# Attention into a routed mixture of experts: the hand-over between the two, and when the token lists of the experts are fetched

## The chip, the cores and the metric

One core of a Trainium2 chip runs the whole program. The metric is device time in microseconds; the times shown are three runs of the kernel before and one further execution under the profiler, from which all rows below are taken.

## The reference, cut to what matters

Attention with rotary positions over 8 batches, 8 heads, 576 tokens and 64 values per head gives 4608 rows of 512. Each row then goes to one of 8 experts, the one with the largest gate logit:

```python
q_rot, k_rot = rotate(q), rotate(k)
scores = matmul(q_rot, k_rot.T) / sqrt(64); attn = softmax(scores)
x = matmul(attn, v)                            # 4608 rows of 512
logits = x @ w_gate; e_idx = argmax(logits, 1) # 8 experts
gate_w = softmax(logits)[row, e_idx]
eom = sigmoid(x @ w_output_gate)
for e in range(8):
    mask = e_idx == e
    h = maximum(x[mask] @ w1[e], 0)            # 512 -> 1024
    out[mask] = gate_w[mask] * eom[mask, e] * (h @ w2[e])
```

## The kernel before, in words

**Attention.** The work goes over 32 pairs of heads (4 pairs in each of 8 batches). A pair has 9 steps g; each makes a block of scores (`scores`, L464 and L457, into the two buffers `sc`), its maximum (`peak`, L470 on VectorE), the exponential (`exp`, L479 on ScalarE) and a transpose (`turn`, L485 on VectorE). The product with v (`values`, L507 into `acc`), its copy (`evict`, L514 to L516), the turn back into rows together with the gate logits (`back`, L522) and the division (`divide`, L530 to L539, into `xb`) follow at fixed distances from the pair's first step, by the table EVENTS; there is one `acc` for all pairs. `att.at(g, k, f)` puts a function at step g, phase k, and `rest(cond)` runs what is left over after the last score step.

**Routing.** When a batch is finished, `place` finds each token's expert and its place in that expert's list: one-hot rows (`oh`, `ohb`), running sums over the token blocks (`ohs`, L620), a matrix product that counts (`s14`, L655), and two masks (`ro` on VectorE, `pl` on GpSimd, L685 and L687) whose product (`s20`, L695) adds token numbers into `lists` (`s21`, L698). The rows of x go to DRAM (`store`, L638 and L640, on the SP queue). For the last batch these functions come as a list of pieces.

**Experts.** The rows of the experts are worked in slots of 256 rows ("double") or 128 ("single"). Slots 0 to 4 are filled from the first six batches and can start before the last two are placed; list 0 gives their rows (`table0`), list 2 the next double slots and list 1 the single ones (`table1`). A list goes through the same function `slots`: it computes a row number, fetches the list by an indirect DMA from DRAM (L794, into `0tk`, `2tk`, `1tk`), waits some pieces, corrects it on VectorE (L801 to L804), turns it on TensorE (L808, `0tr`, `2tr`, `1tr`) and copies it to `idx` (L809). `gather` (L942, GpSimd queue) then fetches the rows of a slot into `xg`.

A slot has 8 steps j. In steps 0 to 3 TensorE multiplies the turned rows `xt` with a quarter of w1 (`products`, L1002, into `ph`, one of two buffers) and `first` takes the relu on ScalarE (L1019) and its low part on VectorE (L1020) into `ht`. In steps 4 to 7 it multiplies `ht` with a quarter of w2 (`second`, L1045, into `py`). Every weight block is split in two parts six steps ahead of its use (`split`: `wh` on ScalarE, L964, `wl` on VectorE or for some blocks GpSimd, L966), and loaded eight ahead (`load`, L955, SP queue). `turn` turns the rows of the next slot (L980 to L983) in steps 4 and 5; `store` scales and scatters the result (L1054 to L1057, GpSimd queue).

**Order.** Every engine runs its instructions in the order in which they are written. The left-over pieces of routing and of `table1` are put between the steps of the slots, two per step:

```python
left = att.last + pieces(moe.table1(), 60)
...
for _ in range(per):        # per = 2
    if left:
        left.pop(0)()
```

At the hand-over the kernel before turns the rows of slot 0 and makes its first two products once the `values` of the last pair (31) are written, then runs the rest of attention, then closes attention's pools and opens the experts' left pools. `ht` lies in the left pool, so `first` of steps 0 and 1 can only be written after that.

Of the kernel before, what the change touches and what calls it, by code (L numbers as in the profile page):

```python
# [117 lines left out]
def body(ctx, tc, nb, offs, qk, v, rope, cst, gates, w, out):  # L118
# [61 lines left out]
    if n0:  # L180
        g = att.done(nb - 3) + 1
        for k, f in enumerate(pieces(moe.table0(), 18)):
            att.at(g + k, 2, f)
        att.at(g + 18, 2, moe.fetch)
# [12 lines left out]
    if not n0:  # L197
        att.rest(lambda g: True)
        main.close()
        moe.open_right(pool(ctx, "mr", 1, side="right", reuse_waits="tile"))  # L200
        left = []
    else:

        att.rest(lambda g: g <= att.G + 1)
        for u in range(3):
            moe.split(u)
        att.rest(lambda g: g <= att.G + 8)
        for h in range(2):
            moe.turn(0, h)
        for j in range(2):  # L210
            moe.products(0, j)
        att.rest(lambda g: True)
        main.close()
    moe.open_left(pool(ctx, "ml", 1, side="left", reuse_waits="tile"),
                  pool(ctx, "ps_m", 1, space=PSUM, side="left", reuse_waits="tile"))
    if n0:
        left = att.last + pieces(moe.table1(), 60)
    else:
        for f in att.last + pieces(moe.table1(), 60):
            f()  # L220
        moe.fetch()
        moe.begin0()
        moe.begin1()
# [8 lines left out]
class Attention:  # L232
# [91 lines left out]
    def step(self, g):  # L324
        G, pairs = self.G, self.pairs
        part = lambda g: (pairs[g // 9], g % 9)
        if g < G:
            pr, i = part(g)
            if i == 0:
                pr.begin()  # L330
            pr.scores(i)
            pr.peak(i)
            pr.exp(i)
        self.now(g, 1)
        if 0 <= g - TURN < G:
            pr, i = part(g - TURN)
            pr.turn(i)
        self.now(g, 2)
        self.now(g, 3)
# [209 lines left out]
def place(tc, pools, pairs, b, NT, cc, trib, oneb, cnt, xbs, xd, row, lists):  # L549
# [155 lines left out]
    if last:  # L705
        return [s0, s1, s2, s3, s4, s5, s6, s7, lambda: (s8(), add0()), both(s9, 1), both(s10, 2), both(s11, 3), both(s12, 4),
                lambda: (s13(), stores(), base()), no, s14, no, s14b, s15, s16, s17, no] + [lambda c=c: ones(c) for c in range(NCH)] + [
                no, no, s20, no, s21, no]

# [15 lines left out]
class Moe:  # L725
# [3 lines left out]
    def __init__(self, tc, nb, pools, cc, ident, cnt, w, xd, lists, lst, out):  # L729
# [5 lines left out]
        self.idx, self.ei = {}, {}  # L735
        self.wr, self.wp, self.xt, self.ht, self.gss, self.pys, self.hrs, self.regs, self.phs = ({} for _ in range(9))

# [27 lines left out]

    def slots(self, n, m, ends, delta, first, step, wait):

# [36 lines left out]
        V.tensor_tensor(out=tk, in0=tk, in1=g, op=ALU.add)  # L804
        yield
        tr = self.small.tile(f"{n}tr2")
# [35 lines left out]
    def table0(self):  # L842
# [13 lines left out]
        yield  # L856
        yield from self.slots(0, 2 * self.n0, end, dl, None, 2, 5)

    def table1(self):
# [25 lines left out]
        if self.n2:  # L885
# [6 lines left out]
            d2 = self.starts("d2", g2, 0.0)  # L892
            yield from self.slots(2, 2 * self.n2, end, d2, g2[:, 0:1], 2, 5)
            yield
# [12 lines left out]
        d1 = self.starts("d1", g1, BIG)  # L907
        yield from self.slots(1, self.n1, e1, d1, g1[:, 0:1], 1, 5)
        self.used = t([1, 1], "used", I32)
# [47 lines left out]
    def split(self, u):  # L957
# [9 lines left out]
        self.wp[u] = (wh, wl)  # L967

    def turn(self, s, h):
        nc, V = self.nc, self.nc.vector  # L970
# [6 lines left out]
        xth, xtl = self.xt[s]  # L977
        tp = self.small.tile(f"mtp{s}_{h}{self.nm}")
        for dc in range(4):
            nc.tensor.transpose(out=tp[:, dc, :], in_=self.xgs[s % 2][:, h, dc * P:dc * P + P], identity=self.ident)  # L980
        hs = slice(h * P, h * P + P)
# [3 lines left out]
    def products(self, s, j):  # L985
        nc = self.nc
        xth, xtl = self.xt[s]
        wh, wl = (a.rearrange("p (d f) -> p d f", f=256) for a in self.wp.pop(8 * s + j))
        ph = self.phs[s, j] = self.ph.tile([P, 2, SLOT], F32, tag=f"ph{j % 2}", name=f"ph{s}_{j}{self.nm}")
        if self.todo[s][0] == 1:  # L990
            n = 0
            for dc in range(4):
                for st, mv in ((xth, wh), (xtl, wh), (xth, wl)):
                    nc.tensor.matmul(ph[:, 0, :], st[:, dc, 0:P], mv[:, dc, :], start=(n == 0), stop=(n == 11))  # L994
                    n += 1
            return
        for f in range(2):
            n = 0
            for dc in range(4):
                fs = slice(f * P, f * P + P)  # L1000
                for st, mv in ((wh, xth), (wh, xtl), (wl, xth)):
                    nc.tensor.matmul(ph[:, f, :], st[:, dc, fs], mv[:, dc, :], start=(n == 0), stop=(n == 11))  # L1002
                    n += 1

    def first(self, s, j):
        nc = self.nc
        fl = lambda a: a.rearrange("p a b -> p (a b)")
        if j == 0:
            self.ht[s] = [self.buf(f"ht{i}", 0, 1, 0, [P, 8, SLOT], F32R, f"ht{i}_{s}{self.nm}") for i in range(2)]
        hth, htl = self.ht[s]  # L1010
        js = slice(2 * j, 2 * j + 2)
        if (s, j) not in self.phs:
            self.products(s, j)
        ph = self.phs.pop((s, j))
        if self.todo[s][0] == 1:
# [68 lines left out]
    def slot(self, s, left, per=2):  # L1084
        for j in range(8):
            u = 8 * s + j
            single = self.todo[s][0] == 1
            if j < 4:
                self.first(s, j)
            else:  # L1090
                self.second(s, j - 4)
# [8 lines left out]
            if j == 6:  # L1100
                self.gather(s + 2)
            for _ in range(per):
                if left:
# [64 lines left out]
```

## Time and profile before

| | us |
|---|---|
| three runs | 1106.68, 1104.14, 1101.99 (median 1104.14) |
| the profiled execution | 1111.51 |
| its span, first to last instruction | 1109.7 |
| TensorE busy in the span | 1027.9 (93%) |
| VectorE busy | 827.9 (75%) |
| ScalarE busy | 644.7 (58%) |
| GpSimd busy | 604.1 (54%) |

Attention takes the first 575 us or so; the slots of the experts start at about 590. The share of busy time is an average over both; what counts in a stage is the wait that ends last there. The chain that ended last is 65% TensorE by its share of the span.

### The profile page before, as it was taken

The numbers are of one execution on the slowest core, as the hardware profiler recorded it, in microseconds if no ns is written. First come the engines' busy times: TensorE is split into PE (matmuls) and PEld (weight loads), VectorE is DVE, ScalarE is ACT, GpSimd is POOL, SyncE is SP. The second block draws the span as 40 slices with busy tenths as digits, with TensorE's granted clock in tenths as the row PEclk, the third lists the DMA queues.
The fourth block names the chain that finished last, engine by engine and source line by source line (L and its number), as shares of the span: only waits on it lengthen the run. The fifth ranks groups of instructions, "written<-read, shape, count | busy, mean of one in ns | idle before, by whom it ended". The sixth has DMA issues, their size and how long they took to land.

```text
span 1109.7 us, 34896 instructions
## 1 busy us (share of the span) xinstructions
PE 1027.9 (93%) x14465; PEld 890.5 (80%) x14465; DVE 827.9 (75%) x1357; ACT 644.7 (58%) x1345; POOL 604.1 (54%) x592
## 2 busy tenths in 40 slices
PE   3999999999999999999976998899999999999995
PEld 3788877877877787787766987798899889889885
DVE  6788888888888688788764775656767867876782
ACT  3466666666666465566453553455757756766772
POOL 4667887887978688688531051112532632632621
PEclk9999999999999899899888998999999999999998
DMA  5545555555746455545266585556887888888870
GB/s 184 162 129 164 167 165 145 152 166 159 199 126 174 114 167 173 130 145 159 51 184 210 199 302 184 190 171 193 301 291 252 286 286 292 265 305 304 256 274 27
DMA packets 58562, 216.48 MB, mean 195 GB/s; under 512 B 9405, under 2 KB 10012, under 8 KB 54304
## 3 DMA queue, kind: packets, MB, share of 16 engines
q1 hardware_dynamic: 50304, 194.03, 55.9%
q0 software_dynamic: 6496, 18.92, 4.8%
q8 instruction: 115, 1.88, 0.7%
q10 hardware_dynamic: 1600, 1.26, 0.4%
q14 instruction: 47, 0.39, 0.1%
HBM read 196.04 MB, written 20.24 MB: 195 GB/s over the span
## 4 chain that ended last, share of the span: by engine, by line
PE 65%; DVE 12%; issue 10%; DMA 6%; ACT 4%; POOL 2%; SPq 1%; POOLq 0%; ACTq 0%; DVEq 0%
PE py L1045 15%; PE sc L464 15%; PE acc L507 14%; PE ph L1002 11%; PE ph L994 4%; DVE m L470 3%; DVE pt L485 3%; DMA out<-y,0idx 3%; ACT pm L479 2%; PE acc L522 2%; PE sc L457 2%; PE mtp L980 1%; DVE wl L966 1%; DMA v<-in_v 1%; DVE xb L530 1%
## 5 line engine op out<-in xcount | busy, mean ns | idle before, releaser
L479 ACT ACTIVATE pm<-sc,m 128x576 f32<-128x576 f32 x288 | 213.5, 741 | 192.9 <-DVE m L470 191.3
L966 DVE TENSOR_TENSOR wl<-wr,wh 128x1024 fp32r<-128x1024 f32 x183 | 254.6, 1403 | 48.1 <-ACT wh L964 46.5
L470 DVE TENSOR_REDUCE m<-sc 128x1 f32<-128x576 f32 x288 | 213.2, 740 | 85.8 <-PE sc L464 70.7
L464 PE MATMUL sc<-kh,q 64*128 64x288 f32 x1024 | 227.7, 330 | 26.4 <-ACT pm L479 11.7
L507 PE MATMUL acc<-pt,v 32*64 32x160 f32 (+1 forms) x9216 | 203.0, 303 | 19.2 <-DMA v<-in_v 5.2
L485 DVE STREAM_TRANSPOSE pt<-pm 128x576 f32<-128x576 f32 x288 | 220.0, 764 | 0.3 <-ACT pm L479 0.3
L1045 PE MATMUL py<-wh,ht 128*128 128x512 f32 x640 | 214.9, 400 | 0.0
L964 ACT CAST wh<-wr 128x1024 fp32r<-128x1024 f32 x208 | 212.7, 1050 | 0.4 <-DMA wr<-in_w 0.4
L464 PEld LDWEIGHTS sc<-kh,q 64*128 64x128 f32 x1024 | 154.1, 195 | 69.5 <-ACT pm L479 26.1
L507 PEld LDWEIGHTS acc<-pt,v 32*64 32x64 f32 x9216 | 163.2, 135 | 43.8 <-issue 21.3
L1002 PE MATMUL ph<-xt,wh 128*128 128x256 f32 x896 | 166.4, 289 | 7.3 <-DVE ht L1020 5.8
L413 POOL TENSOR_TENSOR raw<-raw,rt 128x1152 f32<-128x1152 f32 x62 | 164.1, 2647 | 8.3 <-DMA raw<-in_qk 8.0
L1002 PEld LDWEIGHTS ph<-xt,wh 128*128 128x128 f32 x896 | 143.7, 197 | 9.7 <-issue 6.1
L1045 PEld LDWEIGHTS py<-wh,ht 128*128 128x128 f32 x640 | 120.6, 188 | 24.8
L1002 PE MATMUL ph<-xt,wl 128*128 128x256 f32 x448 | 128.5, 287 | 0.0
L1045 PE MATMUL py<-wl,ht 128*128 128x512 f32 x320 | 125.7, 393 | 0.0
L966 POOL TENSOR_TENSOR wl<-wr,wh 128x1024 fp32r<-128x1024 f32 x25 | 61.3, 2450 | 110.6 <-ACT wh L964 108.2
L464 PE MATMUL sc<-kl,q 64*128 64x288 f32 x512 | 112.6, 302 | 0.6 <-issue 0.6
L417 POOL TENSOR_TENSOR raw<-raw 128x576 f32<-128x576 f32 x62 | 88.1, 1421 | 2.4
L1019 ACT ACTIVATE ht<-ph 128x512 fp32r<-128x512 f32 x56 | 33.5, 598 | 96.1 <-PE ph L1002 96.1
L1002 PEld LDWEIGHTS ph<-xt,wl 128*128 128x128 f32 x448 | 88.6, 198 | 0.0
L464 PEld LDWEIGHTS sc<-kl,q 64*128 64x128 f32 x512 | 86.0, 196 | 0.9 <-issue 0.9
(245 smaller groups left out, 1329.3 us busy)
## 6 DMA issues: line engine op xcount, KB each, us to landing
wr<-in_w SPq DMA_DIRECT2D x208, 512.0 KB, 5.5
raw<-in_qk SPq DMA_DIRECT2D x64, 576.0 KB, 4.7
v<-in_v SPq DMA_DIRECT2D x128, 288.0 KB, 5.2
xd<-xb SPq DMA_DIRECT2D x16, 513.0 KB, 4.9
xd<-xb SPq DMA_DIRECT2D x8, 128.2 KB, 4.3
rt<-in_rope ACTq DMA_DIRECT2D x1, 576.0 KB, 5.6
xg<-xd,2idx POOLq DMA_INDIRECT x18, 6.8
out<-y,2idx POOLq DMA_INDIRECT x18, 5.2
```

Of the source, the lines that this page charges most:

```text
L413: self.eng(eng).tensor_tensor(out=rv, in0=rv, in1=self.rt[:, 2 * t:2 * t + 2, x], op=ALU.mult)
L417: self.eng(eng).tensor_tensor(out=r[:, 2 * t, x], in0=r[:, 2 * t, x], in1=r[:, 2 * t + 1, x], op=ALU.add)
L464: nc.tensor.matmul(ps[:, a, :HS], self.q[r, w, c * P:c * P + P], mov[r, a * HS:a * HS + HS], start=(n == 0), stop=(n == 2))
L470: nc.vector.tensor_reduce(self.m[i], ps[:, :, :HS], axis=AX.XY, op=ALU.max, negate=True)
L479: nc.scalar.activation(pe.rearrange("p (a b) -> p a b", a=2), self.ps[i][:, :, :HS], AF.Exp, bias=self.m[i], scale=1.0, accum_out=self.z[: ...
L485: self.nc.vector.transpose(out=self.pt[:, st[0] + 5 * st[1] if st else 4, :], in_=self.pc.pop(i))
L507: nc.tensor.matmul(self.acc[h * D:h * D + D, a, o:o + 32 * n], self.v[r, h, j, :], self.pt[r, u:u + n, 32 * j:32 * j + 32], start=(j == 0) ...
L964: self.nc.scalar.copy(wh, r)
L966: eng.tensor_tensor(out=wl, in0=r, in1=wh.bitcast(F32), op=ALU.subtract)
L994: nc.tensor.matmul(ph[:, 0, :], st[:, dc, 0:P], mv[:, dc, :], start=(n == 0), stop=(n == 11))
L1002: nc.tensor.matmul(ph[:, f, :], st[:, dc, fs], mv[:, dc, :], start=(n == 0), stop=(n == 11))
L1045: self.nc.tensor.matmul(py[h], st[:, f, hs], mv, start=(f == 0 and n == 0), stop=(f == 7 and n == 2))
```

## The change

It does seven things. `ht` goes to the right pool. The turns of slot 0's rows (`turned_in`, split off from `turn`) go ahead of and behind the `back` of pair 30. `first` of steps 0 and 1 is written out at the hand-over, step 0 ahead of the `back` of pair 31, step 1 after it, and slot 0 leaves them out; in those two steps it runs one piece each, not two. The turn of list 0 moves one piece on, behind the next block of scores (phase 0). The last batch's `place` has 7 pieces fewer, and its stores to DRAM come later in the list. For lists 2 and 1, `slots` waits 7 pieces for the fetched list instead of 5, and 4 pieces between the correction and the turn instead of 1; `table1` is cut into 72 pieces instead of 60.

```diff
-        for k, f in enumerate(pieces(moe.table0(), 18)):
-            att.at(g + k, 2, f)
+        for k, f in enumerate(pieces(moe.table0(), 19)):
+            att.at(g + k, 2 if k < 18 else 0, f)
...
+        moe.turned_in(0, 0)
         att.rest(lambda g: g <= att.G + 1)
+        moe.turned_in(0, 1)
+        for h in range(2):
+            moe.turn(0, h)
         for u in range(3):
             moe.split(u)
         att.rest(lambda g: g <= att.G + 8)
-        for h in range(2):
-            moe.turn(0, h)
-        for j in range(2):
-            moe.products(0, j)
+        moe.first(0, 0)
         att.rest(lambda g: True)
         main.close()
+        moe.first(0, 1)
...
-        left = att.last + pieces(moe.table1(), 60)
+        left = att.last + pieces(moe.table1(), 72)
...
             pr.exp(i)
+        self.now(g, 0)
         self.now(g, 1)
...
-        return [s0, s1, s2, s3, s4, s5, s6, s7, lambda: (s8(), add0()), both(s9, 1), both(s10, 2), both(s11, 3), both(s12, 4),
-                lambda: (s13(), stores(), base()), no, s14, no, s14b, s15, s16, s17, no] + [lambda c=c: ones(c) for c in range(NCH)] + [
-                no, no, s20, no, s21, no]
+        run = lambda *fs: lambda: [f() for f in fs]
+        return [s0, run(s1, s2), s3, run(s4, s5), run(s6, s7), run(s8, add0), both(s9, 1), lambda: [add(c) for c in (2, 3, 4)],
+                run(s10, s11, s12), run(s13, base), no, s14, no, s14b, run(s15, s16, s17)] + [
+                lambda c=c: ones(c) for c in range(NCH)] + [stores, no, s20, no, s21, no]
...
-        yield
+        for _ in range(after):
+            yield
         tr = self.small.tile(f"{n}tr2")
...
-        yield from self.slots(0, 2 * self.n0, end, dl, None, 2, 5)
+        yield from self.slots(0, 2 * self.n0, end, dl, None, 2, 5, 2)
...
-            yield from self.slots(2, 2 * self.n2, end, d2, g2[:, 0:1], 2, 5)
+            yield from self.slots(2, 2 * self.n2, end, d2, g2[:, 0:1], 2, 7, 4)
...
-        yield from self.slots(1, self.n1, e1, d1, g1[:, 0:1], 1, 5)
+        yield from self.slots(1, self.n1, e1, d1, g1[:, 0:1], 1, 7, 4)
...
+    def turned_in(self, s, h):
+        tp = self.tps[s, h] = self.small.tile(f"mtp{s}_{h}{self.nm}")
+        for dc in range(4):
+            self.nc.tensor.transpose(out=tp[:, dc, :], in_=self.xgs[s % 2][:, h, dc * P:dc * P + P], identity=self.ident)
...
-            self.ht[s] = [self.buf(f"ht{i}", 0, 1, 0, [P, 8, SLOT], F32R, f"ht{i}_{s}{self.nm}") for i in range(2)]
+            self.ht[s] = [self.buf(f"ht{i}", 0, 1, 1, [P, 8, SLOT], F32R, f"ht{i}_{s}{self.nm}") for i in range(2)]
...
             if j < 4:
-                self.first(s, j)
+                if s or j > 1 or not self.n0:
+                    self.first(s, j)
...
-            for _ in range(per):
+            for _ in range(per if s or j > 1 else 1):
```

**ScalarE at the hand-over**, from the copy of pair 31's `acc` on (`wh` a weight block's first part, `ht` the relu of `ph`, `xb` the division). Before:

```order
L514 COPY ac_10166<-acc_10013 128x512
L515 COPY ac_10166<-acc_10013 64x64
L516 COPY ac_10166<-acc_10013 64x64
L982 CAST xt_0_10170<-mtp_0_10174 128x4x128
L982 CAST xt_0_10170<-mtp_1_10181 128x4x128
L539 ACTIVATE xb_9306<-acc_10013,rz_114 64x64 x2
L964 CAST wh_10274<-wr_9973 128x1024
L964 CAST wh_10278<-wr_10266 128x1024
L964 CAST wh_10282<-wr_10268 128x1024
L1019 ACTIVATE ht_0_10286<-ph_0_10188 128x512
L964 CAST wh_10290<-wr_10270 128x1024
L1019 ACTIVATE ht_0_10286<-ph_1_10213 128x512
```

In the changed kernel:

```order
L517 COPY ac_10184<-acc_10031 128x512
L518 COPY ac_10184<-acc_10031 64x64
L519 COPY ac_10184<-acc_10031 64x64
L1028 ACTIVATE ht_0_10188<-ph_0_10190 128x512
L542 ACTIVATE xb_9306<-acc_10031,rz_114 64x64 x2
L1028 ACTIVATE ht_0_10188<-ph_1_10239 128x512
L969 CAST wh_10280<-wr_9973 128x1024
L969 CAST wh_10284<-wr_10272 128x1024
L969 CAST wh_10288<-wr_10274 128x1024
L969 CAST wh_10292<-wr_10276 128x1024
L969 CAST wh_10309<-wr_10278 128x1024
```

The two relus now stand ahead of the splits of blocks 3 to 7, the first of them ahead of the division too, and the copies to `xt` have gone to an earlier place.

**TensorE around `s14` of the last batch** (`ohs` the running sums, `oneb` the matrix of ones). Before:

```order
L1045 MATMUL py_1_10404<-wh_10311,ht_0_10286 128x512
L1045 MATMUL py_1_10404<-wl_10312,ht_0_10286 128x512
L1045 MATMUL py_1_10404<-wh_10311,ht_0_10287 128x512
L655 LDWEIGHTS oneb
L655 MATMUL pl_2_10530<-ohs_10436,oneb 128x48
L656 LDWEIGHTS trib
L656 MATMUL pl_2_10530<-ohb_10399,trib 128x40
L1002 MATMUL ph_0_10535<-xt_1_10423,wh_10351 128x256
L1002 MATMUL ph_0_10535<-xt_1_10424,wh_10351 128x256
```

In the changed kernel:

```order
L1054 MATMUL py_1_10409<-wh_10292,ht_0_10188 128x512
L1054 MATMUL py_1_10409<-wl_10293,ht_0_10188 128x512
L1054 MATMUL py_1_10409<-wh_10292,ht_0_10189 128x512
L658 LDWEIGHTS oneb
L658 MATMUL pl_2_10500<-ohs_10405,oneb 128x48
L659 LDWEIGHTS trib
L659 MATMUL pl_2_10500<-ohb_10399,trib 128x40
L1054 MATMUL py_0_10408<-wh_10309,ht_0_10188 128x512
L1054 MATMUL py_0_10408<-wl_10310,ht_0_10188 128x512
```

The count has moved from the end of slot 0 to one step ahead of it: the 12 products with block 7 now come after it.

**GpSimd's queue around the fetch of list 2.** Before:

```order
L687 TENSOR_SCALAR pl_10692<-row,lo_10650,tok_10656 128x128 x5
L942 DMA xg<-xd,0idx 128x513 x2
L1057 DMA out<-y_10808,0idx 4608x512 x2
L942 DMA xg<-xd,0idx 128x513 x2
L790 MEMSET 2tk 18x128
L1057 DMA out<-y_11118,0idx 4608x512 x2
L794 DMA 2tk<-lst_85,2ri 18x128
L942 DMA xg<-xd,2idx 128x513 x2
```

In the changed kernel:

```order
L690 TENSOR_SCALAR pl_10590<-row,lo_10581,tok_10587 128x128 x5
L947 DMA xg<-xd,0idx 128x513 x2
L1066 DMA out<-y_10818,0idx 4608x512 x2
L794 MEMSET 2tk 18x128
L798 DMA 2tk<-lst_85,2ri 18x128
L947 DMA xg<-xd,0idx 128x513 x2
L1066 DMA out<-y_11122,0idx 4608x512 x2
L947 DMA xg<-xd,2idx 128x513 x2
```

The fetch of list 2 now stands ahead of the gather of slot 4 and of slot 2's two stores; the fetch of list 1 keeps its place behind slot 3's stores.

## Rows read from the trace of the kernel before

**Rows 1.** Stages: us; busy PE, PEld, DVE, ACT, POOL; granted clock; DMA share; GB/s.

```profile
566.00:570.00 4.00, 4.00 (x88) 3.40 (x88) 1.44 (x2) 0.83 (x2) 3.08 (x4) 0.57 0.68 194
...
605.80:610.70 4.90, 4.84 (x23) 4.87 (x24) 4.70 (x5) 1.55 (x3) 4.37 (x3) 0.50 0.92 323
...
770.00:1060.00 290.00, 286.88 (x1873) 258.80 (x1872) 217.11 (x232) 199.41 (x293) 126.34 (x71) 1.00 0.82 283
```

**Rows 2.** Who TensorE waited for, 540 to 740 us: total, times, longest.

```profile
PE ph L1002 <- DVE ht L1020: 5.8, 1, 5.8
PE 2tr L808 <- DVE 2tk L804: 5.0, 1, 5.0
PE 1tr L808 <- DVE 1tk L804: 3.8, 1, 3.8
...
PE sc L464 <- DVE 0idx L809: 1.1, 1, 1.1
PE ph L1002 <- ACT xt L982: 1.1, 1, 1.1
PE 0tr L808 <- DVE 0tk L804: 0.9, 1, 0.9
```

**Rows 3.** Timeline around list 0's turn: start, duration, instruction, idle before it.

```profile
547.79 1.64 PE L507 MATMUL acc<-pt,v 32*64 32x160 f32 x80
...
564.81 0.74 ACT L479 ACTIVATE pm<-sc,m 128x576 f32<-128x576 f32 x1 [1.17 <-DVE m L470]
...
566.50 2.97 PE L507 MATMUL acc<-pt,v 32*64 32x160 f32 x80
...
569.40 0.75 PE L464 MATMUL sc<-kh,q 64*128 64x288 f32 x2
```

**Rows 4.** Timeline of TensorE, from the last `values` to slot 1.

```profile
588.61 1.09 PE L980 MATMUL mtp<-ident,xg 128*128 128x128 f32 x8
...
597.33 1.02 PE L695 MATMUL acc<-ro,pl 128*128 128x288 f32 x5
598.28 1.77 PE L522 MATMUL acc<-ii,ac 128*128 128x160 f32 x10
...
613.74 0.39 PE L1045 MATMUL py<-wh,ht 128*128 128x512 f32 x1
...
625.62 0.20 PE L655 MATMUL pl<-ohs,oneb 128*128 128x48 bf16 x1
```

**Rows 5.** Timeline of ScalarE and VectorE in the same stretch.

```profile
601.57 2.93 ACT L964 CAST wh<-wr 128x1024 fp32r<-128x1024 f32 x3
...
602.64 2.36 DVE L966 TENSOR_TENSOR wl<-wr,wh 128x1024 fp32r<-128x1024 f32 x2 [0.48 <-ACT wh L964]
...
604.40 0.59 ACT L1019 ACTIVATE ht<-ph 128x512 fp32r<-128x512 f32 x1
...
605.02 0.69 DVE L1020 SCALAR_TENSOR_TENSOR ht<-ph,ht 128x512 fp32r<-128x512 f32 x1
...
622.51 1.22 DVE L966 TENSOR_TENSOR wl<-wr,wh 128x1024 fp32r<-128x1024 f32 x1
...
623.75 0.12 DVE L620 TENSOR_TENSOR ohs<-ohs,ohb 128x8 bf16<-128x8 bf16 x1
```

**Rows 6.** The chain that ended last: start, duration, what.

```profile
687.73 5.32 PE ph L1002 x24
...
705.02 8.49 PE ph L1002 x72
...
717.55 5.42 PE ph L1002 x24
```

**Rows 7.** GpSimd's masks beside a split, and the first gathers' time to land.

```profile
638.51 5.77 POOL L687 TENSOR_SCALAR pl<-row,lo,tok 128x128 fp32r<-128x128 bf16 x5 [4.70 <-DVE tok L677]
639.00 1.23 DVE L966 TENSOR_TENSOR wl<-wr,wh 128x1024 fp32r<-128x1024 f32 x1
...
xg<-xd,0idx POOLq DMA_INDIRECT x4, 4.0
```

More of the change, by code (lines that the diff above doesn't have):

```diff
@@ L216, in body @@
     if n0:
-        left = att.last + pieces(moe.table1(), 60)
+        left = att.last + pieces(moe.table1(), 72)
     else:
-        for f in att.last + pieces(moe.table1(), 60):
+        for f in att.last + pieces(moe.table1(), 72):
             f()
@@ L735, in __init__ @@
         self.idx, self.ei = {}, {}
-        self.wr, self.wp, self.xt, self.ht, self.gss, self.pys, self.hrs, self.regs, self.phs = ({} for _ in range(9))
+        self.wr, self.wp, self.xt, self.ht, self.gss, self.pys, self.hrs, self.regs, self.tps = ({} for _ in range(9))
         self.T = max(1, self.n1 - 3)
@@ L764, in sums, with slots @@
         return a[:, 4:]
-    def slots(self, n, m, ends, delta, first, step, wait):
+    def slots(self, n, m, ends, delta, first, step, wait, after):
         V, t = self.nc.vector, self.t
@@ L977, in turn @@
         xth, xtl = self.xt[s]
-        tp = self.small.tile(f"mtp{s}_{h}{self.nm}")
-        for dc in range(4):
-            nc.tensor.transpose(out=tp[:, dc, :], in_=self.xgs[s % 2][:, h, dc * P:dc * P + P], identity=self.ident)
+        if (s, h) not in self.tps:
+            self.turned_in(s, h)
+        tp = self.tps.pop((s, h))
         hs = slice(h * P, h * P + P)
@@ L988, in products @@
         wh, wl = (a.rearrange("p (d f) -> p d f", f=256) for a in self.wp.pop(8 * s + j))
-        ph = self.phs[s, j] = self.ph.tile([P, 2, SLOT], F32, tag=f"ph{j % 2}", name=f"ph{s}_{j}{self.nm}")
+        ph = self.ph.tile([P, 2, SLOT], F32, tag=f"ph{j % 2}", name=f"ph{s}_{j}{self.nm}")
         if self.todo[s][0] == 1:
@@ L995, in products @@
                     n += 1
-            return
+            return ph
         for f in range(2):
@@ L1003, in products @@
                     n += 1
+        return ph
     def first(self, s, j):
@@ L1008, in first @@
         if j == 0:
-            self.ht[s] = [self.buf(f"ht{i}", 0, 1, 0, [P, 8, SLOT], F32R, f"ht{i}_{s}{self.nm}") for i in range(2)]
+            self.ht[s] = [self.buf(f"ht{i}", 0, 1, 1, [P, 8, SLOT], F32R, f"ht{i}_{s}{self.nm}") for i in range(2)]
         hth, htl = self.ht[s]
         js = slice(2 * j, 2 * j + 2)
-        if (s, j) not in self.phs:
-            self.products(s, j)
-        ph = self.phs.pop((s, j))
+        ph = self.products(s, j)
         if self.todo[s][0] == 1:
```

## The prediction

> **What bounds the kernel now.** I read four views in this order: busy time by stage, who TensorE waited for, the timeline of the engines around those waits, and the chain that ended last. From 770 us on, TensorE is busy 286.88 of 290 us at the full clock [rows 1], so nothing there is to be had. The waits between 540 and 740 us are another matter: 5.8 us for the relu of slot 0's first product, 5.0 us for list 2, 3.8 us for list 1, and about 2 us around list 0's turn [rows 2]. After each of them the engine runs at the lower of its two levels: 0.57 of full speed on average from 566 to 570 us and 0.50 from 605.8 to 610.7 us [rows 1], and the chain shows 24 products in 5.32 and 5.42 us behind the two list waits, where 72 take 8.49 us at full speed, that is 2.83 us for 24 [rows 6]. So a wait costs its length and about 2.5 us more. TensorE sets the end in this stretch, and all behind it moves with it.
>
> **The change part by part.** The sum is made against the profiled execution, 1111.5 us (span 1109.7); the median of the runs is 7.4 us below it, and I take the same saving from it.
>
> *List 0's turn behind scores.* Before, the 80 products with v start at 566.50, take 2.97 us at a falling clock, and the next scores start at 569.40 [rows 3]. In the changed order one block of scores fills the wait for VectorE, and the turn then waits only for the `sc` buffer, that is for the exponential that ends at 564.81 + 0.74 = 565.55. With 0.25 us for the turn and 1.64 us for 80 products at full clock [rows 3] the next scores start at 567.45: **1.9 us** saved. If the clock falls all the same, the 1.33 us between 2.97 and 1.64 stay and 0.6 us is left; that is one bound, 3 us the other. The gathers are issued 0.8 us later, for the index is copied one maximum later.
>
> *Turns of slot 0 beside `back`.* 8 turns of 1.09 us in all [rows 4] go into the two pauses that TensorE has on both sides of pair 30's `back`, while it waits for ScalarE's copies; they cost nothing there as long as the rows have landed (4.0 us after issue [rows 7], with some 2 us to spare). Their old place is gone, and with it the 1.1 us wait for `xt` [rows 2].
>
> *The hand-over.* From 588.61, where the last `values` end, to 625.62, where slot 1 is about to start, 37.0 us go by [rows 4]. The work of TensorE in it, at full clock: four products of 2.83 us [rows 6] are 11.3 us; the lists' product and `back`, from 597.33 to 598.28 + 1.77, 2.7 us [rows 4]; the second half of slot 0 with the turns of slot 1, from 613.74 to 625.62, 11.9 us [rows 4]. Together 25.9 us. The rest, 11.1 us, is waiting, lower clock and the turns now done before. What is late next? The first relu no longer stands behind the splits on ScalarE, so `ph` is free at once. But the splits of blocks 3 to 7 still stand behind the second relu, and so behind the second product, which ends at 588.6 + 2.8 + 2.7 + 2.8 = 597.0. ScalarE begins them at about 597.7 and not at 601.57 [rows 5]: VectorE, which begins 1.07 us later [rows 5], comes 3.9 us earlier, while TensorE wants everything 9 to 11 us earlier. Block 3 costs TensorE 0.2 us of waiting. The dear one is `s14`, which now stands one step earlier, ahead of the last 12 products, and needs the fourth running sum. Before, VectorE needed from 602.64 to 623.87 for it, 21.2 us [rows 5]. The new order takes out of this stretch two relu parts of 0.69, two splits of 1.22 [rows 5] and a turn's low part of the relu's size, 4.5 us, and a part of its idle time (0.48 us stands in one row; I take 1.2 us in all). That leaves 15.5 us: 598.7 + 15.5 = 614.2. TensorE reaches `s14` at 597.0 + 5.7 + 0.2 and three quarters of 11.9, or 611.8. The new wait is **2.4 us**; from below it is 0, if VectorE has no idle time at all and its small operations overlap, from above 3.5 us, if none of the idle time goes. So the hand-over takes 25.9 + 0.2 + 2.4 = 28.5 us instead of 37.0: **8.5 us** saved, between 6 and 11.
>
> *List 2.* Its fetch stood behind slot 2's two scatters on GpSimd's queue, the second of which waits for the first to land. It now stands two steps before the slot's end (a step is 11.9 / 4 = 3 us), ahead of a gather and both scatters, and the turn is where it was, in step 2 of slot 3. Its index row must be ready for that; it is written by VectorE in the same step, and GpSimd waits there, but behind it only the gather of slot 4 is queued, which is wanted more than 20 us later. So the correction finds the list landed some 10 us before, and the wait of 5.0 us and its 5.32 − 2.83 = 2.5 us of lower clock go: **7.5 us**.
>
> *List 1.* The fetch keeps its place; the turn comes three steps later, 9 us against a wait of 3.8 us. With 5.42 − 2.83 = 2.6 us of clock: **6.4 us**. If a scatter takes 3 us longer than here nothing is lost. Both lists together I bound by 10 and 14 us.
>
> *Shorter placing, later stores.* Seven pieces fewer bring `s20`, the masks' product, to step 4 of slot 1. The masks on GpSimd take 5.77 us [rows 7] and end about a microsecond before TensorE wants them; I count nothing, from above 1.5 us of new wait, from below nothing. Beside the masks VectorE's split takes 1.23 us [rows 7], its usual time, so the other mask is ready in time too. The Trainium skill (SBUF — State Buffer, SBUF: two separate sides) has an exclusive pair of ports for GpSimd and a VectorE operation with two SBUF inputs, where the loser "fully blocks": by it two splits would each wait for one mask of 1.15 us, `s20` would come 1 us late, and the saving below would be 23.3 us; the trace does not show this here, and the row decides. The stores leave SP's queue later, so weight loads stop waiting behind them; TensorE waits for no load there [rows 2], so nothing is counted.
>
> The sum: 1.9 + 8.5 + 7.5 + 6.4 = **24.3 us**. 1111.5 − 24.3 = 1087.2 for a profiled execution, and 1104.1 − 24.3 = **1079.8 us** for the median.
>
> **Rivals.**
> 1. *The new wait lowers the clock, and VectorE becomes the bound of slots 0 and 1.* For it: list 0's waits of 0.9 and 1.1 us [rows 2] were enough for 0.57 [rows 1], and 2.4 us is near the 3.8 us that were followed by half speed. Against it: TensorE is busy without a pause before this wait, which it was not at list 0. Price: 2.5 us of clock, 1 us more for `s14`, 1 us at `s20`: 1084. The Trainium skill (TensorE: Matmul & The Clock Gate, The HAM clock gate) calls the half rate the default, released by activity; the four stretches agree, and by it this rival is as open as the rows leave it.
> 2. *No new wait.* VectorE's small operations pack well and the running sums are ready: 2.4 us more saved, 1077; with the full 3 us at list 0, 1076.
> 3. *The change does not do what it says for a list.* If the fetch of list 2 or 1 still lands late, because GpSimd's queue is blocked by its index row or by scatters, about half of 13.9 us stays: 1087, or with both, 1094.
> 4. *The gain is given back later.* Past 770 us the DMA share is 0.82 at 283 GB/s [rows 1]; were the weights the limit, the time would stay near 1104. Against it: TensorE stands still for only 3.1 us in 290.
> 5. *Slower.* The turns of slot 0 now stand ahead of `back` in TensorE's order, behind the gathers. If these land late, each microsecond delays everything behind it by one. It would have to be over 24 us, with a landing of some 30 us instead of 4.0 [rows 7], to make the kernel slower than before: 1110 at 36 us.
>
> **How the numbers follow.** Forecast 0.53, rival 1 0.24, rival 2 0.13, rival 3 0.05, rival 4 0.03, rival 5 0.02. The predicted time is the forecast's, 1079.8 us. The low end, 1073.5: 1104.1 less 24.3, 2.4 (no wait at `s14`), 1.1 (list 0's bound), and 2.8 for the scatter of the runs. The high end, 1089.5: a saving of 24.3 less 2.6 (clock), 1.1 and 1.5 (waits), 1.3 (list 0) is 17.8, 1086.3, and 3 us of scatter. Both hold the first three cases. A measurement can tell about 0.5% from no change, 5.5 us: rivals 1 to 3 are all faster by more. Faster 0.95, same 0.03, slower 0.02.
>
> **What would show it.** Right: the waits for `2tk`, `1tk` and for `ht` in slot 0 are gone, their stretches at half speed too; slot 1 starts 10 us earlier; a new wait of some 2.4 us stands at the count of the last batch, for `ohs`. Wrong: that wait is over 4 us or followed by half speed, the masks' product or the turns of slot 0 wait for GpSimd, or the stretch past 770 us is longer than before.

## The result, and the profile after

| | before | changed |
|---|---|---|
| median of four runs, us | 1103.07 (1101.19 to 1106.68) | 1092.16 (1087.53 to 1093.89) |
| profiled execution, its span, us | 1111.51, 1109.7 | 1092.42, 1090.6 |

The ratio is 0.9872, 95% interval 0.9838 to 0.9907: the changed kernel is faster, by 10.9 us between the medians or 14 us by the ratio, and not by the 24.3 us of the sum. 1092.2 lies 2.7 us above the high end of the range. A second set of runs on another chip gave 0.9912 (0.9878 to 0.9945), 11.5 us. Ratios and intervals, here and below, leave out slow runs, those over 1.5% above the fastest of their kernel; the medians have all runs.

The page of the changed kernel:

```profile
span 1090.6 us, 34893 instructions
...
PE 1018.6 (93%) x14465; PEld 880.0 (81%) x14465; DVE 826.7 (76%) x1357; ACT 644.1 (59%) x1345; POOL 607.0 (56%) x592
```

TensorE is busy for 9 us less and the span is 19 us shorter, so about half of what the profiled execution saves was idle time. Whom TensorE waited for between 540 and 740 us (total, times, longest), the view of [rows 2]:

```profile
PE pl L698 <- POOL pl L690: 3.2, 3, 1.4
PE pl L658 <- DVE ohs L623: 2.8, 1, 2.8
PE acc L510 <- issue: 2.6, 2, 2.2
...
PE 0tr L813 <- ACT pm L482: 0.9, 1, 0.9
...
PE ph L1012 <- issue: 0.6, 1, 0.6
```

The three waits of 3.8 to 5.8 us at the head of [rows 2] are gone. In their place stand the count of the last batch (L658), the masks' product (L698, called `s20`) and time put down to issue, in which the engine waits for nothing that the profile shows.

To place the difference, both timelines are cut at the last maximum of pair 31 (VectorE, `m`) and at ScalarE's scaling of each slot's result (`y`, the end of slots 0, 1, 4 and 5). Before:

```profile
573.58 0.73 DVE L470 TENSOR_REDUCE m<-sc 128x1 f32<-128x576 f32 x1
...
625.14 0.69 ACT L1054 ACTIVATE y<-py,gs 128x512 f32<-128x512 f32 x1 [2.33 <-PE py L1045]
...
649.76 0.69 ACT L1054 ACTIVATE y<-py,gs 128x512 f32<-128x512 f32 x1 [3.45 <-PE py L1045]
...
734.64 0.69 ACT L1054 ACTIVATE y<-py,gs 128x512 f32<-128x512 f32 x1 [2.38 <-PE py L1045]
...
757.93 0.69 ACT L1054 ACTIVATE y<-py,gs 128x512 f32<-128x512 f32 x1 [2.42 <-PE py L1045]
```

Changed:

```profile
568.93 0.76 DVE L473 TENSOR_REDUCE m<-sc 128x1 f32<-128x576 f32 x1 [0.80 <-PE sc L467]
...
616.07 0.69 ACT L1063 ACTIVATE y<-py,gs 128x512 f32<-128x512 f32 x1 [1.48 <-PE py L1054]
...
646.53 0.68 ACT L1063 ACTIVATE y<-py,gs 128x512 f32<-128x512 f32 x1
...
716.47 0.69 ACT L1063 ACTIVATE y<-py,gs 128x512 f32<-128x512 f32 x1 [2.77 <-PE py L1054]
...
739.30 0.69 ACT L1063 ACTIVATE y<-py,gs 128x512 f32<-128x512 f32 x1 [2.33 <-PE py L1054]
```

| from | to | before | changed | saved | forecast |
|---|---|---|---|---|---|
| pair 31, fifth maximum | last maximum | 9.6 | 10.5 | -0.9 | 1.9 |
| last maximum | end of slot 0 | 51.6 | 47.1 | 4.4 | 8.5 |
| end of slot 0 | end of slot 1 | 24.6 | 30.5 | -5.8 | 0 |
| end of slot 1 | end of slot 4 | 84.9 | 69.9 | 14.9 | 13.9 |
| end of slot 4 | end of slot 5 | 23.3 | 22.8 | 0.5 | 0 |

Slots 2 to 4 hold both lists. That makes 13.1 us, and 0.5 us follow past slot 5. The other 5.5 of the 19.1 us between the two profiled executions lie ahead of pair 30, where nothing was changed: the way from the first maximum of pair 0 to that of pair 30 took between 517.1 and 525.9 us in the fourteen traces of this study, whatever the kernel. Such a swing is as large as most experiments' effect, and a median of four runs doesn't average it out. So I judge the experiments by **the stretch**, from the last maximum of pair 31 to the end of slot 5: 184.4 us before, 170.4 changed. It repeats well: 184.8 and 171.4 us in second traces of the same kernels on another chip.

**List 0.** TensorE in the changed kernel, around list 0's turn, at the last `values` and first product, and at the count:

```profile
560.18 0.22 PE L813 MATMUL 0tr<-ident,0tk 10*128 10x10 f32 x1 [0.94 <-ACT pm L482]
560.33 3.09 PE L510 MATMUL acc<-pt,v 32*64 32x160 f32 x80
...
565.75 2.17 PE L510 MATMUL acc<-pt,v 32*64 32x160 f32 x64
...
580.39 3.30 PE L510 MATMUL acc<-pt,v 32*64 32x160 f32 x101 [2.19 <-issue]
584.15 0.89 PE L510 MATMUL acc<-pt,v 32*64 32x128 f32 x13 [0.46 <-issue]
...
588.80 0.39 PE L1012 MATMUL ph<-xt,wl 128*128 128x256 f32 x1 [0.56 <-issue]
...
613.63 0.20 PE L658 MATMUL pl<-ohs,oneb 128*128 128x48 bf16 x1 [2.77 <-DVE ohs L623]
```

The turn no longer waits for VectorE's correction, but the 80 products behind it take 3.09 us, not the 1.64 us at full clock of [rows 3]. The granted clock is 0.50 from 560.7 to 567.5 us here, and was from 566.5 to 569.9 us before. Granted clock by stretch (the columns of [rows 1]):

```profile
563.40:567.80 4.40, 4.40 (x78) 3.94 (x76) 2.60 (x6) 1.09 (x3) 2.73 (x6) 0.53 0.68 189
581.60:588.00 6.40, 5.94 (x81) 5.12 (x66) 0.54 (x4) 0.90 (x3) 0.00 (x0) 0.50 0.98 310
607.00:613.00 6.00, 3.85 (x19) 2.83 (x17) 5.81 (x20) 3.88 (x7) 0.00 (x0) 1.00 0.87 317
635.90:639.20 3.30, 3.30 (x9) 2.54 (x9) 0.00 (x0) 0.00 (x0) 1.95 (x2) 0.50 0.79 248
```

The 2.77 us at the count leave the clock at 1.00. That is not so in every execution: nine traces of this study have this wait, at 2.76 to 2.85 us, and in four of them the clock falls there. One is the changed kernel's second trace (after_again), where the wait ends at 617.96 us:

```profile
617.60:620.90 3.30, 2.94 (x9) 2.36 (x10) 3.16 (x10) 1.31 (x2) 0.00 (x0) 0.50 0.80 237
```

In those four traces the second half of slot 0 takes 16.6 to 17.6 us, in the other five 15.1 to 15.2 us. Behind the waits at `s20` the changed kernel's clock is 0.50, and twelve products that take 2.8 us at full clock take 4.4.

**The masks.** GpSimd, from slot 0's two scatters on:

```profile
617.03 1.09 POOL L1066 DMA_INDIRECT out<-y,0idx  x1 [10.66 <-ACT y L1063]
626.75 0.99 POOL L1066 DMA_INDIRECT out<-y,0idx  x1 [8.62 <-DVE ro L688]
627.78 7.76 POOL L690 TENSOR_SCALAR pl<-row,lo,tok 128x128 fp32r<-128x128 bf16 x5
```

VectorE had written what the masks need by 623.9, but they stand behind the second scatter, which follows the first by 9.7 us; then they take 7.76 us where [rows 7] has 5.77.

### The profile page after: what moved, and what is told of

Read it like the earlier page. It is cut to its first block, busy times and chain, and to the rows that moved or that the text cites. A ratio compares the mean times of both kernels' runs of the same rounds, so it can differ in the third digit from the quotient of the medians.

```text
span 1090.6 us, 34893 instructions
## 1 busy us (share of the span) xinstructions
PE 1018.6 (93%) x14465; PEld 880.0 (81%) x14465; DVE 826.7 (76%) x1357; ACT 644.1 (59%) x1345; POOL 607.0 (56%) x592
## 4 chain that ended last, share of the span: by engine, by line
PE 71%; DVE 13%; issue 7%; ACT 6%; DMA 1%; POOL 1%; ACTq 0%; POOLq 0%; DVEq 0%
PE py L1054 18%; PE sc L467 15%; PE acc L510 15%; PE ph L1012 13%; PE ph L1004 4%; DVE m L473 4%; DVE pt L488 3%; ACT pm L482 3%; PE acc L525 2%; DVE wl L971 2%; PE mtp L977 1%; DVE xb L533 1%; PE sc L460 1%; ACT xb L542 1%; ACT wh L969 1%
## 5 line engine op out<-in xcount | busy, mean ns | idle before, releaser
L510 PE MATMUL acc<-pt,v 32*64 32x160 f32 (+1 forms) x9216 | 200.8, 301 | 21.5 <-issue 5.7
L510 PEld LDWEIGHTS acc<-pt,v 32*64 32x64 f32 x9216 | 161.2, 134 | 46.1 <-issue 22.9
L1012 PE MATMUL ph<-xt,wh 128*128 128x256 f32 x896 | 159.6, 282 | 0.0
L1012 PEld LDWEIGHTS ph<-xt,wh 128*128 128x128 f32 x896 | 138.6, 190 | 2.3 <-issue 0.7
L1012 PE MATMUL ph<-xt,wl 128*128 128x256 f32 x448 | 126.1, 281 | 0.6 <-issue 0.6
L1012 PEld LDWEIGHTS ph<-xt,wl 128*128 128x128 f32 x448 | 85.4, 191 | 0.8 <-issue 0.8
```

The source lines that it names most:

```text
L510: nc.tensor.matmul(self.acc[h * D:h * D + D, a, o:o + 32 * n], self.v[r, h, j, :], self.pt[r, u:u + n, 32 * j:32 * j + 32], start=(j == 0) ...
```

## The experiments

Every kernel but before_again is the changed one with the edit shown. The first four, the second four and the last four shared a chip each, with the kernel before beside them.

| kernel | median, us | ratio to before (95%) | fifth to last maximum, us | the stretch, us |
|---|---|---|---|---|
| s14_later | 1088.9 | 0.9824 (0.9767 to 0.9881) | 8.5 | 165.9 |
| s20_later | 1090.0 | 0.9869 (0.9809 to 0.9928) | 10.7 | 165.9 |
| masks_first | 1090.8 | 0.9865 (0.9815 to 0.9915) | 9.0 | 165.7 |
| list0_undone | 1093.0 | 0.9876 (0.9808 to 0.9943) | 9.6 | 171.3 |
| loads_held | 1085.8 | 0.9770 (0.9687 to 0.9852) | 10.9 | 167.5 |
| held_s14 | 1089.3 | 0.9856 (0.9783 to 0.9928) | 10.6 | 161.1 |
| turns_undone | 1096.9 | 0.9921 (0.9877 to 0.9964) | 10.6 | 174.5 |
| lists_undone | 1093.6 | 0.9903 (0.9872 to 0.9934) | 10.5 | 169.8 |
| stores_later | 1095.1 | 0.9872 (0.9831 to 0.9913) | 15.4 | 174.5 |
| after_again | 1098.5 | 0.9912 (0.9878 to 0.9945) | 15.5 | 171.4 |
| best_again | 1087.8 | 0.9796 (0.9762 to 0.9829) | 14.0 | 161.2 |
| before_again | one run, 1116.8 | - | 14.0 | 184.8 |

**s14_later: the count one step later.**

```diff
-                run(s10, s11, s12), run(s13, base), no, s14, no, s14b, run(s15, s16, s17)] + [
-                lambda c=c: ones(c) for c in range(NCH)] + [stores, no, s20, no, s21, no]
+                run(s10, s11, s12), run(s13, base), no, no, no, s14, s14b] + [
+                lambda c=c: ((s15(), s16(), s17()) if c == 0 else None, ones(c)) for c in range(NCH)] + [stores, no, s20, no, s21, no]
```

> Against the changed kernel at 1092.2 us, whose trace has TensorE wait 2.8 us at the last batch's count (s14) for the running sums. Here the count is one step later again, at the end of slot 0. Theory (the missing gain went into waits that the change itself makes): the 2.8 us go, slot 1 starts 2.8 us earlier, and the masks' wait at s20 stays about 3.2 us, because it hangs on slot 0's second scatter, which moves with the end of slot 0: 1089.4. Rival (VectorE sets the place): s20 waits 2.8 us longer, 6 us, and the time stays at 1092.

The wait at the count is gone. So is the one at `s20`, which neither theory had: the stretch is 4.5 us shorter, not 2.8. GpSimd shows why:

```profile
619.76 1.03 POOL L1066 DMA_INDIRECT out<-y,0idx  x1 [9.07 <-ACT y L1063]
625.26 1.05 POOL L1066 DMA_INDIRECT out<-y,0idx  x1 [4.48 <-DMA out<-y,0idx]
627.39 6.01 POOL L690 TENSOR_SCALAR pl<-row,lo,tok 128x128 fp32r<-128x128 bf16 x5 [1.08 <-DVE tok L680]
```

The second scatter follows the first by 5.5 us instead of 9.7, and the masks take 6.01 us. In the same trace TensorE stood still for 3.55 us inside slot 0's first product:

```profile
591.64 0.58 PE L1012 MATMUL ph<-xt,wl 128*128 128x256 f32 x1 [3.55 <-issue]
```

**s20_later: the masks' product one step later.**

```diff
-                lambda c=c: ones(c) for c in range(NCH)] + [stores, no, s20, no, s21, no]
+                lambda c=c: ones(c) for c in range(NCH)] + [stores, no, no, no, s20, s21]
```

> Only the masks' product s20 is one step (2.9 us) later; the list pieces behind it keep their places. Theory (waits of the change's own making): the split wait of 3.2 us for the masks falls under 0.5 us, and the stretch at half clock behind it (1.7 us) goes: 4.4 us less than the changed kernel, 1087.8. Rival (the clock falls there for another reason, and the end is set elsewhere): y1 at most 1 us earlier, 1091 to 1092.

Of the 3.2 us, 0.5 is left, and the stretch is 4.5 us shorter against 4.4 expected:

```profile
PE pl L658 <- DVE ohs L623: 2.8, 1, 2.8
PE ph L1012 <- issue: 2.3, 1, 2.3
...
PE pl L698 <- POOL pl L690: 0.5, 2, 0.4
```

**masks_first: slot 0's second scatter behind the masks on GpSimd's queue.**

```diff
-            nc.gpsimd.indirect_dma_start(
+            put = lambda h=h: nc.gpsimd.indirect_dma_start(
...
+            if (s, h) == (0, 1) and not self.nm:
+                self.late = put
+            else:
+                put()
...
         left = att.last + pieces(moe.table1(), 72)
+        left[21] = lambda: moe.late()
```

> Slot 0's second scatter is written behind the five masks on GpSimd's queue; s14 and s20 stay. Theory 1 (queue: the masks wait for the scatter, which waits for the first scatter to land): the masks start at about 624 instead of 627.8 us, are done by 631.6 even at 1.55 us each, the wait at s20 and the half clock behind it go: 4.5 us less than the changed kernel, 1087.7. Theory 2 (contention: VectorE's work beside them slows the masks): they now lie wholly beside VectorE's five ro, take over 1.55 us each, up to 2.2, end at 635, and half of the wait stays: 1090.

The masks start at 622.74 us, the wait at `s20` is gone and the stretch is 4.7 us shorter (4.5 expected of theory 1). So the queue made the wait. The masks' length tells the second cause. VectorE's splits (`wl`) while each of the five masks ran, its busy time being the third of the columns behind the length; in the changed kernel:

```profile
627.78:629.32 1.54, 1.08 (x3) 0.47 (x4) 0.86 (x1) 0.00 (x0) 1.00 0.99 391
629.32:630.11 0.79, 0.39 (x1) 0.28 (x2) 0.08 (x1) 0.00 (x0) 1.00 1.09 290
630.11:632.95 2.84, 0.40 (x1) 0.10 (x1) 2.27 (x2) 0.00 (x0) 1.00 0.79 232
632.95:634.76 1.81, 0.00 (x0) 0.00 (x0) 1.22 (x1) 0.00 (x0) 1.00 0.89 333
634.76:635.54 0.78, 0.00 (x0) 0.00 (x0) 0.00 (x0) 0.00 (x0) 1.00 0.96 352
```

and with the masks first:

```profile
622.74:623.54 0.80, 0.65 (x3) 0.41 (x3) 0.04 (x1) 0.00 (x0) 1.00 0.59 131
623.54:625.37 1.83, 1.40 (x6) 1.00 (x6) 1.17 (x1) 0.00 (x0) 1.00 1.03 381
```

A mask takes 0.79 us with no split beside it, 1.8 with one and 2.84 with two: each split holds GpSimd up by about 1.03 us and keeps its own 1.2 us. The roles can be exchanged: in the changed kernel a split that GpSimd does itself (599.39 to 602.08 us) begins ahead of one on VectorE, and that one takes 2.87 us:

```profile
600.29 2.87 DVE L971 TENSOR_TENSOR wl<-wr,wh 128x1024 fp32r<-128x1024 f32 x1 [0.49 <-ACT wh L969]
```

The five `ro`, which theory 2 suspected, cost the masks nothing. In the changed kernel the masks begin so late that the splits of slot 1's later steps, which are not spaced by `ro` any more, fall on them.

**list0_undone: list 0's turn ahead of the scores again** (18 pieces, all in phase 2, one piece between correction and turn).

> List 0's turn back in its old place, ahead of the scores. My prediction's step: 1.9 us slower than the changed kernel, 1094.1. The trace of the changed kernel says the opposite: there the stretch lost 0.9 us against before, because the lower clock lasted twice as long: 1091.3. Rival: the two orders cost the same within 0.5 us, 1092, and the length at half clock is chance.

From the fifth to the last maximum it takes 9.6 us, 0.9 less than the changed kernel and as much as before. The prediction's 1.9 us are not there: with list 0's turn behind the scores, this piece takes 8.5 to 10.9 us in eight traces (the last chip aside), and 9.6 less 1.9 would be 7.7. But as it varies that much in kernels that leave list 0 alone, the 0.9 us don't tell the reading of the trace from the rival. From the first maximum of pair 30 to the fifth of pair 31 it is 24.85 to 24.95 us in thirteen of the fourteen traces, before and changed: VectorE's pace hides the turn up to there.

**loads_held: weight blocks 4 and up wait for slot 0's first relu.**

```diff
+            self.nc.sync.dma_start(out=self.lst[1][0:1, 0:4], in_=self.ht[0][0].bitcast(F32)[0:1, 0, 0:4])
         self.more(0)
```

> The changed kernel, but SyncE issues weight blocks 4 and up only once the relu of slot 0's first product has begun to write ht (a DMA of 4 values from ht stands ahead of them on its queue). Theory (TensorE's own instruction blocks come late while the weights fill the DMA engines, and the waits that hid this before are gone): the idle time put down to issue between 575 and 592 us, 5 to 6 us in the four experiments, falls to 1 us or less; slot 1 starts 4 to 5 us earlier against pair 31; 1087.5. Rival A (the stalls come with the number of instructions, whatever else is loaded): they stay at 5 us and the time at 1092. Rival B (the weights are needed that early): ScalarE's splits of blocks 4 to 7 wait for them, the gain is given back, 1092 to 1095.

From 580 to 590 us the DMA share (the last but one column) falls from about 1.03 to 0.04 and 0.17; first the changed kernel, then this one:

```profile
580.00:585.00 5.00, 4.15 (x115) 3.33 (x115) 2.14 (x10) 0.19 (x1) 0.00 (x0) 0.62 1.02 204
585.00:590.00 5.00, 4.44 (x26) 4.24 (x25) 0.00 (x0) 0.90 (x3) 0.00 (x0) 0.70 1.03 410
```

```profile
580.00:585.00 5.00, 5.00 (x124) 4.52 (x119) 1.62 (x9) 1.08 (x4) 0.00 (x0) 0.66 0.04 6
585.00:590.00 5.00, 5.00 (x36) 4.30 (x35) 1.27 (x2) 0.60 (x1) 0.00 (x0) 1.00 0.17 37
```

The stall inside slot 0's first product is gone and the stretch 2.9 us shorter, but the 2.2 us inside the last `values` stay. Half of the theory holds. From the last `values` to the end of that product, the three traces with the loads held (this one, held_s14 and best_again) have 2.1 to 2.2 us put down to issue, and the eight others with slot 0's turns in their new place 3.2 to 6.3. The trace's packet records agree for the part that went: with the masks first TensorE stalls from 583.41 to 585.95 us, and a 16 KB packet of the instruction queue is under way from 583.61 to 584.69. For the part that stayed, the DMA share was still 0.73 from 575 to 580 us here (the stores of batch 6), so it isn't settled whether load or the number of instructions makes it. On the last chip that stall was 3.7 and 4.2 us (after_again, stores_later) and 2.1 with the loads held (best_again), so there load made a part of it.

**held_s14: both edits together.**

> The loads held and s14 one step later, together. Theory: the two gains lie in different stretches, the wait at s14 is under 1 us and the masks' wait at s20 stays gone as with s14 alone (about 6 us less there from pair 31 to the end of slot 1), the issue stalls go as well: 1084. Rival (VectorE sets the place of s14, so that what is won ahead of it is waited for there): the wait at s14 returns at 2 to 3 us: 1087 to 1088.

161.1 us, 9.3 less than the changed kernel; neither the count nor `s20` is waited for. The median, 1089.3 us, sits in the swing of attention: this kernel's trace spent 524.0 us on the way to pair 30, 4.2 more than the changed kernel's.

**turns_undone: slot 0's turns behind the last `values` again.**

> The turns of slot 0 back behind the last values, as before; all else as changed. My prediction's step: 1.1 us of turns and 1.5 us of waits for xt come back, 2.6 us slower than the changed kernel, 1094.8. Theory (the instruction block is late anyway): the stall of 2.3 to 3.6 us inside slot 0's first product is hidden under these waits and goes, so the time stays within 1 us of the changed kernel, 1092.

4.1 us longer in the stretch, with the median on the same side: 2.6 us pass between the end of the last `values` and the first product, none in the changed kernel; these are the 2.6 us of the prediction's step. The issue stall in the product does go, as the theory said, but half clock takes its place (16.3 us from the first product to slot 0's second half, 16.4 in the changed kernel). Another 1.9 us are lost in slot 0's second half. There the granted clock is 0.50 from 618.4 to 625.3 us, around the end of the wait at the count; as the changed kernel's second trace shows the same without this edit, they can't be put down to it.

**lists_undone: 5 and 1 pieces of waiting again, 60 pieces.**

> Lists 2 and 1 wait 5 and 1 pieces again, table1 in 60 pieces; the hand-over and the shorter placing stay. List 2's fetch still stands ahead of slot 2's scatters, so its turn should wait about 2 us instead of 5; list 1's fetch lands at 705.9 us and its turn would come at 703.7, so it waits about 3 us. With 2.5 us of lower clock behind each wait that is over 2 us: 1092.2 + 2 + 3 + 5 = 1102. Rival 1 (the earlier place of the fetch is all that counts for list 2): no wait there, 1097.7. Rival 2 (no clock drop behind so short a wait): 1097.

No list is waited for, and the stretch is 0.6 us shorter than the changed kernel's: rival 1 was right about list 2, and all three expected list 1's wait back. GpSimd's queue:

```profile
667.57 1.13 POOL L798 DMA_INDIRECT 2tk<-lst,2ri  x1 [9.75 <-issue]
...
673.80 1.03 POOL L1066 DMA_INDIRECT out<-y,0idx  x1 [2.20 <-ACT y L1063]
...
691.05 1.14 POOL L798 DMA_INDIRECT 1tk<-lst,1ri  x1 [10.30 <-DMA wr<-in_w]
...
697.29 1.03 POOL L1066 DMA_INDIRECT out<-y,0idx  x1 [2.21 <-ACT y L1063]
```

With fewer pieces spent on list 2, list 1's fetch too is written ahead of a slot's scatters (697.29, slot 3's first). So for list 2 the place of the fetch is enough, without the longer wait behind it. For list 1 the edit changed both at once. In the changed kernel its fetch (701.25 us) stands behind slot 3's second scatter (699.96), lands at 705.84, and the turn at 711.11 waits for nothing: there it is the later turn that ends the wait. Either is enough.

**stores_later: the last batch's stores two steps later** (`[no, no, s20, no, s21, stores]`).

> The last batch's stores of x to DRAM (1.15 MB) are written five pieces later, two steps behind their place in the changed kernel; nothing else. In the changed kernel SyncE issues them at 616.05 us and GpSimd issues slot 0's first scatter at 617.03; its second follows only 9.7 us after, where with s14 later, the scatter 0.65 us ahead of the stores, it was 5.5 us. Theory (the scatter queues behind the stores in the DMA engines and holds the masks behind it): the gap between the two scatters falls to 5 to 7 us, the masks start at about 624 instead of 627.8, and the wait at s20 with its half clock, 4.5 us, goes: 1087.7. Rival (the weights fill the engines whatever the stores do): gap over 8 us, wait at s20 about 3 us, 1092.

The wait at `s20` stays, 2.9 us, and the scatters lie 9.9 us apart. That is the rival's outcome, but the edit did not separate the two: SyncE issues the stores at 624.12 us and GpSimd the scatter at 624.26, still right behind them. In the three traces in which the scatter is issued 0.65 us ahead of the stores the distance is 5.5, 7.2 and 6.9 us; in the eight of the changed kernel's kind with the stores ahead and the second scatter in its old place it is 8.3 to 10.2. The kernel before, with its stores about 2 us ahead, has 6.7 and 7.7. This is a correlation, and the cause stays open. The stretch is 3.1 us longer than the changed kernel's on the same chip (174.5 against 171.4), with the clock at 0.50 for 13.7 us in slots 0 and 1 against 6.8 there.

**after_again, before_again, best_again: both kernels and the best one on one chip** (best_again is held_s14).

> The changed kernel once more. Theory: the stretch from block 5 of pair 31 to the end of slot 5 takes 180.9 us again within 2 us, with 2 to 4 us of issue stalls, 2.8 us at s14 and 3.2 us at s20; what differs between its executions lies in attention, where 6 us and more come and go ahead of pair 30. Median 1092. Rival (the waits of its first trace were chance): one of the three is missing.

> The kernel before, with a second trace. If the code sets the stretch, block 5 of pair 31 to the end of slot 5 takes 193.9 us again within 2 us, while the way to pair 30 may differ by 6 us, for the first trace lost 6.5 us there between pairs 20 and 24. Rival (the waits of list 2, list 1 and ht were chance): under 190.

> Loads held and s14 one step later, once more, beside the changed kernel on one chip. From its first trace the stretch from block 5 of pair 31 to the end of slot 5 takes 171.7 us against 180.9 in the changed kernel: 9 us less, 1083 if the changed kernel shows 1092. Rival (the gain of the stretch is given back later): within 2 us of the changed kernel.

Counted from the fifth maximum as in the expectations, the times are 186.9, 198.8 and 175.2 us: 6, 5 and 3.5 us above the first traces, outside the 2 us. All of that but 1 us lies between the fifth and the last maximum, where on this chip all four kernels take 14.0 to 15.5 us. There TensorE's weight loads stood idle with nothing to wait for that the profile shows, ten times in the changed kernel between 556 and 575 us (two or three times, 1.2 us at most, in this piece on the other chips), and the clock was at 0.50 for 10 to 17 us:

```profile
PEld acc L510 <- issue: 3.7, 10, 0.5
```

Past it the changed kernel's three waits are back (2.8 at the count, 2.7 at `s20`, 4.1 of issue), the saving in the stretch is 13.4 us (14.0 the first time), and the best kernel saves 10.2 us more. Its waits from 575 to 770 us:

```profile
PE acc L510 <- issue: 2.1, 1, 2.1
PE ph L1012 <- DVE xt L993: 1.3, 1, 1.3
PE acc L510 <- DVE gs L986: 1.2, 1, 1.2
```

Here the medians agree: 1087.8 against 1098.5 us. The best kernel stands at 0.9796 (0.9762 to 0.9829) of the kernel before; its interval and the changed kernel's don't overlap.

## Why the prediction was right, and where its sizes were not

The direction was right, and the removed waits went as described. Of the 24.3 us of the sum 13.1 were there: 2.8 less at list 0, 4.1 less at the hand-over and 5.8 less in slot 1, with 1.0 more in slots 2 to 4 and 0.5 more in slot 5.

- **Both lists, 13.9 us: right** (14.9 with all of slots 2 to 4). For list 1 the reason, "the turn comes three steps later", holds in the changed kernel, whose fetch still stands behind the scatters; lists_undone shows a second way, the fetch ahead of them.
- **Turns of slot 0: right.** Undone, the 2.6 us come back at that place.
- **The hand-over, 8.5 us: mis-sized, 4.4.** The count's wait was forecast as 2.4 us and measured 2.8. The step that failed is "four products of 2.83 us", at full clock: the first took 5.1 us (584.97 to 590.08), at half clock up to 588.0 and with a stall of 0.56, and in s14_later, masks_first, s20_later and list0_undone it held a stall of 2.3 to 3.6 us put down to issue. The 5.1 us are 2.3 of the 4.1 us that are missing; about 1 us more went ahead of them, in the last `values`, where the sum had put nothing. Before, TensorE waited at the first product for `xt` [rows 2], and a packet of the instruction queue came in meanwhile (590.43 to 591.52 us). The cover that I had seen for the turns was, it seems, the cover of this as well: turns_undone brings the wait back and has no stall. loads_held shows that the weights' traffic makes the stall in the product.
- **`s20`, "I count nothing, from above 1.5 us": failed, 5.8 us in slot 1.** 3.2 us of it are the waits and 1.6 the half clock behind them; the turn of the lists, which stands in slot 2 before and in slot 1 now, is in the rest. I had put the masks' end a microsecond ahead of TensorE's need, and had not followed GpSimd's queue: in the changed order the second scatter is what they wait for. masks_first takes it from ahead of them, and 4.7 us are back; s20_later gives 4.5. I also took "the masks 5.77 us" for a fixed length and looked at VectorE's split for a sign of contention, where its usual 1.23 us seemed to rule it out. The masks are what is held up. By the Trainium skill (SBUF — State Buffer, SBUF: two separate sides), of a GpSimd operation that reads SBUF and a VectorE operation with two SBUF inputs the one that starts first keeps the shared ports and the other is blocked. The trace agrees in that one of the two is held up for most of the time that the other runs beside it: here the masks, by 1.03 us a split, and at 600.29 us VectorE's split. Which began first it can't always show: the split of 632.97 us begins 0.02 us after the mask that it holds up. The 5.77 us of [rows 7] already held it: the five masks of the batch before took 3.91 us in the same trace.
- **List 0, 1.9 us: failed, -0.9.** The step that failed is that the scores' start carries over to the end. Up to the fifth maximum of pair 31 VectorE's pace sets the time and nothing is won. The next scores do start 0.5 us sooner, counted from it (4.9 us against 5.4), about the 0.6 us of the bound for a falling clock, but the half clock lasts 6.8 us instead of 3.4 and the last maximum comes 0.9 us later. The bound from below was too high. The size of the loss is within what this piece varies by.

Rival 1 was the nearest: it had the lower clock and a late `s20`, at 1084 us. It put the clock's fall at the count, where the clock stayed at 1.00 in the first trace and fell in the second. What it lacked most is the size of `s20`: masks_first and s20_later give back 4.7 and 4.5 us, and it had 1.

## What to carry to other kernels

When a wait goes, ask of everything that happened during it, instruction blocks included, whether it still has time. Follow the queue of each engine that comes near the end of a step, not only the engine's work: a scatter that waits for another to land holds all that stands behind it. Where executions of one kernel differ by more than the effect, judge by a stretch of the trace between two instructions that bracket the edit, and look at the granted clock in it: one wait was followed by half clock in one execution of a kernel and not in another.

## What the runs showed of the hardware that I had not expected

- A stretch of short products can be followed by idle time put down to issue: 174 products of the last `values` run in 3.23 us, and then TensorE stands still for 2.19 us; with the weights held back it is 2.16. On the last chip it was 3.74 us, and 2.12 with the weights held back.
- GpSimd's mask takes 0.79 us alone and about 1.03 us more for each VectorE split beside it, whose own length stays at 1.2 us in the changed kernel; beside a split that GpSimd had begun first, VectorE's took 2.87 us.
- The length of an idle time did not tell whether the clock falls. The wait at the count, 2.76 to 2.85 us in one piece, left the granted clock at 1.00 in five traces and was followed by 0.50 in four. The waits at `s20`, 1.6 to 3.2 us in two or three pieces, were followed by 0.50 in six traces of seven.
